# Splitting a unit's maxima before they are transposed, and two row DMAs in place of four

## The chip, the cores and the metric

The kernel runs on one core of a Trainium2 chip. The metric is the device time of one execution in microseconds; for the kernel before it is the median of three runs, 1954.19 us (1954.18 to 1955.42). Beside it stands a profiled execution of 1953.52 us, whose trace is read below.

## The reference

Two branches are mixed by a gate that is computed for each of 2048 positions (`S`); the width `D` is 640, with 32 heads of 20.

```python
def reference(A_x, A_wqkv, A_wo, B_x, B_dft_seq_re, B_dft_seq_im, B_dft_hid_re, B_dft_hid_im, gate_w):
    def _A_ref(x, wqkv, wo):
        B, S, D = x.shape
        H = 32
        Dh = D // H
        qkv = (x @ wqkv).reshape(B, S, 3, H, Dh).transpose(2, 0, 3, 1, 4)
        q, k, v = qkv[0], qkv[1], qkv[2]
        scores = jnp.einsum("bhqd,bhkd->bhqk", q, k) * (Dh ** -0.5)
        p = _softmax(scores, axis=-1)
        o = jnp.einsum("bhqk,bhkd->bhqd", p, v)
        return o.transpose(0, 2, 1, 3).reshape(B, S, D) @ wo

    def _B_ref(x, dft_seq_re, dft_seq_im, dft_hid_re, dft_hid_im):
        a = jnp.einsum("bsd,ed->bse", x, dft_hid_re)
        b = jnp.einsum("bsd,ed->bse", x, dft_hid_im)
        return jnp.einsum("ts,bse->bte", dft_seq_re, a) - jnp.einsum("ts,bse->bte", dft_seq_im, b)

    x = A_x
    g = _sigmoid((x * gate_w).sum(-1, keepdims=True))
    a = _A_ref(x, A_wqkv, A_wo)
    b = _B_ref(x, B_dft_seq_re, B_dft_seq_im, B_dft_hid_re, B_dft_hid_im)
    return g * a + (1 - g) * b
```

The inputs `A_wqkv` and `A_wo` are scaled by 64, so the scores are large and the softmax needs the maximum of each row.

## The kernel before

All large products but the attention's probabilities times the values run on TensorE in the type fp32r. To keep precision, an operand is split into two fp32r parts: `split(dst1, dst2, src, e1, e2)` (L98 to 103) copies `src`, rounded, into `dst1` (L100 on ACT, L102 elsewhere) and the rest, `src - dst1`, into `dst2` (L103).

**Units.** The attention is cut into 32 units (`NU`): a pair of heads and one half of the queries (1024). A unit has 32 steps. The keys of a pair of heads lie in `kst`, the queries in `qst`, two buffers each, with head 0 from partition 0 on and head 1 from partition 64 on. A head has 60 partitions (`KROWS`): three times 20, for the products of the two parts. Behind them come two more partitions: in `qst` they hold the negated maximum of each query in two parts, and in `kst` they hold ones. So a matmul over 62 partitions gives score minus maximum, which ACT turns into the exponential.

**The two kinds of score matmul.** An `m` (`s_mm`, L159) computes 128 queries by 512 keys over 60 partitions, only for the maximum: DVE reduces the tile to one column of `mx` (L161). An `e` (L685) computes the transposed scores, 128 keys by 512 queries over 62 partitions, and ACT takes the exponential (L687). The `m` run 41 steps (`LEAD`) ahead of the `e`. All of them, and the transpose below, take the five PSUM banks of `bank()` in turn.

**The order.** After the projections, the work is issued in cycles of four steps by the string `ORDER`, `"emFemFFFFemFeFFmeFFemFFFmmFFmeeB"`: eight `e`, eight `m`, fifteen places `F` and one burst `B`. In an `F` some pieces of other work are issued (`fill`): first the hidden transform (`hid_tile`, matmuls at L301), later the transform over the sequence (`dft_step`, matmuls at L523); `goals` says up to which piece. One `dft_step` is three pieces, and eight of them (24 pieces) use one loaded tile of the transform's matrix (`raw`, L413, from `in_cdft`); every 16th also loads earlier outputs (`yt`, L511). A burst calls `max_nm` for a unit whose maxima are complete, then `run_extras` (reading a finished output tile from `yp`, on ACT at L309 or L542, then on DVE at L310 or L543; loads of `araw`, L428; preparations on POOL), then sixteen matmuls of probabilities with values (`av`, L448), then `max_chain` for that unit.

**Steps and queues.** `begin(i)` opens step i of the `e`: it runs what `at_step` put there, and some stores. `now[0]` is the step of the latest `begin`; it is 4c + 4 in the burst of cycle c. The DMAs of `sp.dma_start` go to SP's queue in the order of the program. SP works through it as fast as the waits of each DMA allow; each DMA also waits for an earlier one to land, whose semaphore it reuses (here the one eight before). `unit_end` stores a unit's results: sums to `l_scr` (L462), back as `lc` (L465), their reciprocals (L468) to `r_scr` (L471), broadcast back as `rb` (L475), a product on POOL (L478) and the store to `o_scr` (L486). That store lies on step 25 of the next unit.

**A unit's maxima before the change.** `max_nm` (L173) reduces `mx`, 128 x 64, to `nm`, 128 x 16: for each of 128 query rows, 2 heads by 8 query tiles, negated (L175). `max_chain` (L190) transposes `nm` on TensorE into a PSUM bank, 16 x 128 (L193), and splits it there on DVE into `m1` and `m2` (L102, L103). Two steps later `rows()` writes for each head one row of 1024 from `m1` (L201) and one from `m2` (L202) into the two partitions of `qst`: four DMAs of 4 KB. For the first unit, whose maxima are computed during the projections, `rows()` follows at once.

Of the kernel before, what the change touches and what calls it, by code (L numbers as in the profile page):

```python
# [10 lines left out]
F32 = mybir.dt.float32  # L11
R = mybir.dt.float32r
AF = mybir.ActivationFunctionType
ALU = mybir.AluOpType
AX = mybir.AxisListType
# [3 lines left out]
P = 128  # L19
# [39 lines left out]
def f32(ap):  # L59
    return ap.bitcast(F32)  # L60
# [3 lines left out]
def mix_kernel(ctx: ExitStack, tc: tile.TileContext, xa, wqk, wb, cdft, wo, out):  # L64
    nc = tc.nc
    pe, act, dve, pool, sp = nc.tensor, nc.scalar, nc.vector, nc.gpsimd, nc.sync
    ctx.enter_context(tc.manual_schedule())

    def pools(**kw):
        return ctx.enter_context(tc.tile_pool(**kw))  # L70

    const = pools(name="const", bufs=1)
    small = pools(name="small", bufs=1)
# [14 lines left out]
    ident = const.tile([P, P], F32, name="ident")  # L88
# [9 lines left out]
    def split(dst1, dst2, src, e1, e2):  # L98
        if e1 is act:
            act.activation(dst1, src, AF.Copy)  # L100
        else:
            e1.tensor_copy(dst1, src)  # L102
        e2.tensor_tensor(dst2, src, f32(dst1), op=ALU.subtract)  # L103
# [8 lines left out]
    def bank():  # L112
        return ps_w.tile([P, 512], F32, name=f"ps{next(turn) % 5}")
# [24 lines left out]
    def q_unit(n):  # L138
        u = n % 2 * (S // 2)
        return qst[n // 2 % 2][:, u : u + S // 2]  # L140

    mx, nms, ends = {}, {}, []
    now, later = [-1], {}

    def at_step(i, fn):
        later.setdefault(i, []).append(fn)
# [16 lines left out]
    def s_end(i):  # L163
        n, s = divmod(i, 32)
        if n < NU and s == 31:
            if now[0] < 0:
                max_nm(n)
            else:
                ends.append(n)
        if s == 1 and 0 < n <= NU and now[0] < 0:  # L170
            max_chain(n - 1)

    def max_nm(n):  # L173
        nms[n] = small.tile([P, 16], F32, name="nm", bufs=2)
        dve.tensor_reduce(nms[n], mx.pop(n).rearrange("p h q c -> p (h q) c"), axis=AX.X, op=ALU.max, negate=True)  # L175

    def s_step(i):
        for fn in [s_mm(i, h) for h in range(2)]:
# [10 lines left out]

    def max_chain(n):  # L190
        q = q_unit(n)
        pt = bank()[:16, :P]
        pe.transpose(pt, nms.pop(n), ident)  # L193
        m1 = small.tile([16, P], R, name="m1", bufs=2)
        m2 = small.tile([16, P], R, name="m2", bufs=2)
        split(m1, m2, pt, dve, dve)

        def rows():
            for h in range(2):
                b = 64 * h + KROWS  # L200
                sp.dma_start(f32(q[b : b + 1, :]), f32(m1[8 * h : 8 * h + 8, :]))  # L201
                sp.dma_start(f32(q[b + 1 : b + 2, :]), f32(m2[8 * h : 8 * h + 8, :]))  # L202

        if now[0] < 0:
            rows()
        else:
            at_step(now[0] + 2, rows)


    pa = pools(name="att", bufs=1)  # L210
# [163 lines left out]
    for n, c in enumerate(order):  # L374
        for t in range(4):
            m = 4 * n + t
# [314 lines left out]
    def burst(c):  # L691
        for n in ends:
            max_nm(n)
        run_extras(max(done - HIDS, 0) // 3, 2)
        for kt in (2 * c, 2 * c + 1):
            av_step(now[0], kt // NS, kt % NS)
        while ends:
            max_chain(ends.pop(0))
        if c == HID - 1:
            start_dft()  # L700
# [91 lines left out]
```

## Time and profile before

| | |
|---|---|
| median of 3 runs | 1954.19 us |
| the profiled execution | 1953.52 us |
| its span, first to last instruction | 1951.7 us |
| mean granted TensorE clock | 0.997 |
| PE busy | 1918.5 us (98%) |
| DVE busy | 1454.1 us (75%) |
| ACT busy | 1211.8 us (62%) |
| POOL busy | 1045.8 us (54%) |

PE is TensorE's matmuls, PEld its weight loads, DVE VectorE, ACT ScalarE, POOL GpSimd, SP the engine whose queue issues most DMAs. A row of a timeline has the start and the duration in us, the engine, the line, the operation, what it writes and reads, the shapes, how many instructions were merged, and in brackets the idle time before it and what ended it. A row of the waits has who waited for whom, the total in us, how often, and the longest. A row of the stretches has the stretch, its length, each engine's busy time with its number of instructions (PE, PEld, DVE, ACT, POOL, or only the first of them where one line was asked for), the granted clock, the share of the DMA engines that was busy, and GB/s. A row of the groups has busy time and the mean duration in ns behind the bar, then the idle time. Ends of matmuls are modelled.

### The profile page before, as it was taken

To read this page: it belongs to the slowest core of one execution; us is meant where nothing else is said; L and a number is where in the kernel's file an instruction comes from. 1 tells how busy PE (TensorE), PEld (TensorE's weight loads), DVE (VectorE), ACT (ScalarE), POOL (GpSimd) and SP (SyncE) were. 2 spreads that over 40 slices of the span, in tenths; PEclk is the share of its full clock that TensorE was granted. 3 is DMA by queue.
4 is the path that set the end of the run, shared out by engine and by line. 5 is a ranking of instruction groups with operands and counts; after the bars stand their busy time and mean duration, and the time that the engine had idled before them with its cause. 6 is when DMAs were issued, how large, how long until landed. Compare 5 with 4: busy or idle time off the path is not lost. (4 is left out here: it accounts for less than half of the span.)

```text
span 1951.7 us, 43695 instructions
## 1 busy us (share of the span) xinstructions
PE 1918.5 (98%) x17080; PEld 1375.4 (70%) x17080; DVE 1454.1 (75%) x2419; ACT 1211.8 (62%) x2337; POOL 1045.8 (54%) x975
## 2 busy tenths in 40 slices
PE   8999999999999999999999999999999999999999
PEld 7987767777775667666666666666666666666679
DVE  4144568889887888888888878888888887888323
ACT  4221147777776676666776766676766776776741
POOL 1210001111005989457469968995786789787512
PEclk9999999999999999999999999999999999999999
DMA  7763321212114584435356746664554565454355
GB/s 224 173 172 127 130 100 46 78 61 74 47 58 141 170 228 152 122 116 149 97 173 199 196 154 189 212 177 123 149 171 125 183 169 181 154 149 147 98 165 179
DMA packets 196414, 281.02 MB, mean 144 GB/s; under 512 B 73272, under 2 KB 137816, under 8 KB 194288
## 3 DMA queue, kind: packets, MB, share of 16 engines
q1 hardware_dynamic: 158992, 246.20, 40.8%
q0 software_dynamic: 37216, 32.03, 6.7%
q8 instruction: 134, 2.20, 0.5%
q14 instruction: 72, 0.59, 0.1%
HBM read 213.81 MB, written 63.70 MB: 142 GB/s over the span
## 5 line engine op out<-in xcount | busy, mean ns | idle before, releaser
L161 DVE TENSOR_REDUCE mx<-ps 128x1 f32<-128x512 f32 x2048 | 1287.4, 683 | 197.4 <-PE ps L159 178.8
L687 ACT ACTIVATE p<-ps 128x512 f32<-128x512 f32 x2048 | 1080.9, 598 | 443.4 <-PE ps L159 241.2
L159 PE MATMUL ps<-kst,qst 60*128 60x512 f32 x2048 | 776.1, 427 | 8.0 <-DVE mx L161 3.2
L685 PE MATMUL ps<-qst,kst 62*128 62x512 f32 x2048 | 700.7, 422 | 5.8 <-DMA qst<-m 4.2
L523 PE MATMUL yp<-a,part 64*128 64x320 f32 x5376 | 687.6, 309 | 0.1
L523 PEld LDWEIGHTS yp<-a,part 64*128 64x128 f32 x5376 | 593.7, 186 | 15.3 <-DVE m L543 0.3
L448 PE MATMUL av<-p,v 128*21 128x512 f32 x4096 | 494.4, 599 | 0.1
L685 PEld LDWEIGHTS ps<-qst,kst 62*128 62x128 f32 x2048 | 335.5, 185 | 215.2 <-DVE mx L161 181.9
L159 PEld LDWEIGHTS ps<-kst,qst 60*128 60x128 f32 x2048 | 364.5, 185 | 38.2 <-DVE mx L161 11.8
L103 POOL TENSOR_TENSOR part<-raw,part 128x1024 fp32r<-128x1024 f32 x112 | 267.2, 2386 | 9.0
L448 PEld LDWEIGHTS av<-p,v 128*21 128x21 f32 x4096 | 98.3, 100 | 226.8 <-issue 223.1
L301 PE MATMUL yp<-wb,xs 64*128 64x320 f32 x1920 | 237.4, 309 | 3.7 <-ACT raw L309 3.5
L301 PEld LDWEIGHTS yp<-wb,xs 64*128 64x128 f32 x1920 | 206.8, 187 | 8.9 <-ACT raw L309 4.1
L419 POOL TENSOR_TENSOR raw<-raw,raw 128x1024 f32<-128x1024 f32 x78 | 187.4, 2402 | 17.3 <-DMA raw<-in_cdft 11.8
L102 POOL CAST part<-raw 128x1024 fp32r<-128x1024 f32 x112 | 116.4, 1039 | 116.8 <-PE yp L523 87.4
L102 POOL CAST wb<-raw 128x966 fp32r<-128x966 f32 (+1 forms) x4 | 3.4, 856 | 215.8 <-PE ps L159 215.8
L554 POOL TENSOR_TENSOR yt<-yt,m 128x320 f32<-128x320 f32 x64 | 55.5, 878 | 111.3 <-DVE m L543 104.2
L478 POOL TENSOR_TENSOR o<-o,rb 128x512 f32<-128x512 f32 x32 | 41.4, 1294 | 134.5 <-DMA rb<-r_scr 73.7
L103 POOL TENSOR_TENSOR a<-araw,a 128x320 fp32r<-128x320 f32 x112 | 97.8, 873 | 9.0
L103 DVE TENSOR_TENSOR p<-ps,p 128x512 fp32r<-128x512 f32 x40 | 27.5, 691 | 94.1 <-ACT p L100 91.4
L106 PE MATMUL ps<-xs,part 128*128 128x512 f32 x200 | 80.2, 401 | 7.8 <-ACT xs L100 6.1
L100 ACT ACTIVATE p<-ps 128x512 fp32r<-128x512 f32 x40 | 23.7, 597 | 101.4 <-PE ps L108 101.4
(67 smaller groups left out, 1331.8 us busy)
## 6 DMA issues: line engine op xcount, KB each, us to landing
raw<-in_cdft SPq DMA_DIRECT2D x192, 512.0 KB
araw<-a_scr SPq DMA_DIRECT2D x192, 160.0 KB
qk_scr<-p SPq DMA_DIRECT2D x40, 512.0 KB
kst<-qk_scr POOLq DMA_DIRECT2D x32, 320.0 KB, 12.3
qst<-qk_scr POOLq DMA_DIRECT2D x64, 160.0 KB, 8.2
a_scr<-raw SPq DMA_DIRECT2D x64, 160.0 KB
yt<-y_scr SPq DMA_DIRECT2D x64, 160.0 KB
y_scr<-yt SPq DMA_DIRECT2D x64, 160.0 KB
```

Source lines behind the costliest of these rows:

```text
L102: e1.tensor_copy(dst1, src)
L103: e2.tensor_tensor(dst2, src, f32(dst1), op=ALU.subtract)
L106: pe.matmul(ps, st1, mv1, start=first, stop=False)
L159: pe.matmul(ps, q[b : b + KROWS, qt * P : (qt + 1) * P], k[b : b + KROWS, kc * 512 : (kc + 1) * 512], start=True, stop=True)
L161: return lambda: dve.tensor_reduce(mx[n][:, h, qt, kc : kc + 1], ps, axis=AX.X, op=ALU.max)
L301: pe.matmul(yp[h][:, :HE], xs[r, xz, d, cs], w[r, wz, d, :HE], start=d == 0 and z == 0, stop=d == ND - 1 and z == 2)
L419: pool.tensor_tensor(raws[0], raws[0], raws[1], op=ALU.add if PRODUCTS[n][0][1][0] > 0 else ALU.subtract)
L448: pe.matmul(av[32 * j : 32 * j + DH + 1, :], v[:, kt, h * (DH + 1) : (h + 1) * (DH + 1)], pp[qc][:, h, :], start=kt == 0, stop=kt == NS - 1)
L523: pe.matmul(yp[h][:, :HE], c[r, cz, cs], a[r, az], start=s == 0 and z == 0, stop=s == NS - 1 and z == 2)
L554: pool.tensor_tensor(y, y, m, op=ALU.add if sg == signs[tt, hf] else ALU.subtract)
L685: pe.matmul(pt, k[b : b + KROWS + 2, kt * P : (kt + 1) * P], q[b : b + KROWS + 2, qc * 512 : (qc + 1) * 512], start=True, stop=True)
L687: act.activation(pts[n, kt, qc][:, h], pt, AF.Exp, scale=float(DH) ** -0.5)
```

## The change

`max_nm` no longer stops at `nm`. It splits it at once on DVE into two parts in a new tile `nms`, laid out per head as first part then second part, 32 columns in all. `max_chain` transposes the 32 columns together into a bank, 32 x 128, and copies the result to SBUF with one DVE instruction, into a tile `m` with one buffer. There the rows of a head, 8 of the first part and 8 of the second, lie next to each other, so one DMA of 8 KB fills both partitions of `qst` for that head. `rows()` is called three steps later in place of two.

```diff
     def max_nm(n):
-        nms[n] = small.tile([P, 16], F32, name="nm", bufs=2)
-        dve.tensor_reduce(nms[n], mx.pop(n).rearrange("p h q c -> p (h q) c"), axis=AX.X, op=ALU.max, negate=True)
+        nm = small.tile([P, 2, 8], F32, name="nm", bufs=2)
+        dve.tensor_reduce(nm, mx.pop(n), axis=AX.X, op=ALU.max, negate=True)
+        nms[n] = small.tile([P, 2, 2, 8], R, name="nms", bufs=2)
+        split(nms[n][:, :, 0], nms[n][:, :, 1], nm, dve, dve)
...
     def max_chain(n):
         q = q_unit(n)
-        pt = bank()[:16, :P]
-        pe.transpose(pt, nms.pop(n), ident)
-        m1 = small.tile([16, P], R, name="m1", bufs=2)
-        m2 = small.tile([16, P], R, name="m2", bufs=2)
-        split(m1, m2, pt, dve, dve)
+        pt = bank()[:32, :P]
+        pe.transpose(pt, f32(nms.pop(n)).rearrange("p h z q -> p (h z q)"), ident)
+        m = small.tile([32, P], F32, name="m")
+        dve.tensor_copy(m, pt)
 
         def rows():
             for h in range(2):
                 b = 64 * h + KROWS
-                sp.dma_start(f32(q[b : b + 1, :]), f32(m1[8 * h : 8 * h + 8, :]))
-                sp.dma_start(f32(q[b + 1 : b + 2, :]), f32(m2[8 * h : 8 * h + 8, :]))
+                sp.dma_start(f32(q[b : b + 2, :]), m[16 * h : 16 * h + 16, :])
 
         if now[0] < 0:
             rows()
         else:
-            at_step(now[0] + 2, rows)
+            at_step(now[0] + 3, rows)
```

## Prediction

> **What bounds the kernel now.** I read the page first, then who waited for whom on PE, then the time of single cycles, and then the timelines around the maxima and around the rows that go into `qst`.
>
> ```profile
> span 1951.7 us, 43695 instructions
> ...
> PE 1918.5 (98%) x17080; PEld 1375.4 (70%) x17080; DVE 1454.1 (75%) x2419; ACT 1211.8 (62%) x2337; POOL 1045.8 (54%) x975
> ```
> ```profile
> PE ps L106 <- ACT xs L100: 6.1, 1, 6.1
> PE ps L685 <- DMA qst<-m: 4.2, 2, 3.3
> ```
>
> PE is busy for 98% of the span, so time is gained only by taking work off PE or by ending one of its few waits. The second view lists them; two of the score matmuls (L685) waited, 4.2 us together, for the very DMAs that this change touches.
>
> Next, what a unit's maxima cost. The first pair of rows is a cycle with the transpose and the next cycle without one; the second pair is the same stretches for the filling matmuls alone.
>
> ```profile
> 1222.80:1229.11 6.31, 6.31 (x60) 4.19 (x60) 5.55 (x12) 4.20 (x8) 6.03 (x9) 1.00 0.47 130
> 1229.11:1235.17 6.06, 6.06 (x57) 4.09 (x56) 4.96 (x9) 4.18 (x8) 5.87 (x4) 1.00 0.65 217
> ```
> ```profile
> 1222.80:1229.11 6.31, 3.31 (x24) 2.72 (x24) 1.00 0.47 130
> 1229.11:1235.17 6.06, 3.27 (x24) 2.77 (x24) 1.00 0.65 217
> ```
>
> Both hold 24 fills, and PE is busy throughout both (its first number equals the length), so the 0.25 us between them is nearly all PE time. Where it goes:
>
> ```profile
> 1222.80 1.92 PE L448 MATMUL av<-p,v 128*21 128x512 f32 x16
> 1224.64 0.28 PE L193 MATMUL ps<-ident,nm 128*16 128x128 f32 x1
> 1224.85 0.49 PE L685 MATMUL ps<-qst,kst 62*128 62x512 f32 x1
> ```
> ```profile
> 1224.02 0.21 DVE L175 TENSOR_REDUCE nm<-mx 128x16 f32<-128x64 f32 x1
> 1224.95 0.28 DVE L102 CAST m<-ps 16x128 fp32r<-16x128 f32 x1 [0.72 <-PE ps L193]
> 1225.27 0.28 DVE L103 TENSOR_TENSOR m<-ps,m 16x128 fp32r<-16x128 f32 x1
> 1225.48 0.67 DVE L161 TENSOR_REDUCE mx<-ps 128x1 f32<-128x512 f32 x1
> ```
>
> The transpose starts at 1224.64 and the next matmul at 1224.85, so its place on PE is 0.21 us, of the 0.25. The two DVE instructions behind it, which the change cuts to one, are covered: PE goes on with the scores and fills while DVE does them. So shortening them gains nothing. A wait is marked before the transpose's weight load, but it is not the reduction's:
>
> ```profile
> 1224.64 0.09 PEld L193 LDWEIGHTS ps<-ident,nm 128*16 128x16 f32 x1 [0.85 <-DVE nm L175]
> ```
> ```profile
> 1026.96 0.18 PEld L685 LDWEIGHTS ps<-qst,kst 62*128 62x128 f32 x1 [0.85 <-DVE mx L161]
> ```
>
> The same 0.85 us stands after the sixteen `av` matmuls in a cycle without a transpose. It is the end of those matmuls; `nm` was finished at 1224.02 + 0.21 = 1224.23, 0.41 us before the load. That 0.41 us is the cover which the change will use.
>
> **The change part by part.**
>
> *The split ahead of the transpose.* Behind the reduction on DVE come a copy and a subtraction of 128x16, each depending on the one before. The trace has neither. The nearest row in shape is the first below; the far bound is the 0.28 us of the same two operations on 16x128 from PSUM, above.
>
> ```profile
> L390 DVE TENSOR_SCALAR gate<-gate 128x16 f32<-128x16 f32 x1 | 0.2, 165 | 0.0
> ```
> ```profile
> 1883.98 1.97 DVE part L103
> 1885.99 0.41 PE ps L108
> ```
>
> Between dependent DVE instructions lie 0.04 us (1224.95 + 0.28 = 1225.23 to 1225.27), and from DVE's end to a PE that waits also 0.04 (1883.98 + 1.97 = 1885.95 to 1885.99, on the chain that ended last). How many units this concerns stands in the waits of the weight loads:
>
> ```profile
> PEld ps L193 <- DVE nm L175: 24.6, 29, 0.8
> ```
>
> At 165 ns each the parts reach PE 0.04 + 0.165 + 0.04 + 0.165 + 0.04 = 0.45 us after the reduction: 0.04 over the cover. At 0.28 it is 0.68, or 0.27 over. Below nothing it cannot be, since the transpose already starts as soon as the `av` matmuls let it. I take 165 ns, which has the shape, and charge the 29 units of that row: 29 x 0.04 = +1.2 us; the far end is 29 x 0.27 = +7.8 us.
>
> Two things are queued behind the new pair. On PE, all of the following scores and fills wait with the transpose; that is what is charged. On DVE, in about a third of the units, it is the reading of a finished output tile:
>
> ```profile
> 1727.23 0.49 DVE L543 TENSOR_TENSOR m<-yp,m 128x320 f32<-128x320 f32 x1
> ```
> ```profile
> 1728.15 0.31 PE L523 MATMUL yp<-a,part 64*128 64x320 f32 x2
> ```
>
> It would start 0.41 later (0.45 less the last handover) and end at 1728.13, and with 0.04 to PE just meet the first fill into that tile at 1728.15. No charge, but the cover is gone too.
>
> *One transpose of 32 columns in place of 16.* The moving side stays 128 wide, so its time stays. The weight load is 0.09 us for 16 columns and 0.18 for 128; 16 more are at most 0.02 us, 32 x 0.02 = 0.6 us if it shows. I take +0.2.
>
> *One copy of 32x128.* DVE loses one instruction of 0.28 us behind the transpose and gains two of 0.165 ahead; the next maximum (L161, 1225.48) may start some 0.3 us earlier. PE waits for neither here, so 0. The bank is released earlier too; nothing waited for it.
>
> *One step later.* `rows()` moves from step now + 2 to now + 3. The burst is at step 32n - 8, so the rows move from 32n - 6 to 32n - 5. Between these two `begin` calls the order string has three F places, which run two or three fill pieces; a fill issues loads only in every 24th piece, and working out `goals` for the 31 later units gives none there. The stores `y_scr` lie on steps divisible by 4, `a_scr` on 32n - 7, and `store_o` on 32n - 7, all on the same side as before. So on SP's queue the rows pass nothing, and on POOL's they never were. SP is not paced by steps; it stops only at what a DMA needs:
>
> ```profile
> SPq L201 <- DVE m L103: 121.6, 25, 10.8
> ...
> SPq L202 <- DMA o_scr<-o: 1.4, 1, 1.4
> ```
>
> In 25 of 32 units SP stands at the rows before the split is done. There the move changes nothing.
>
> *Two DMAs for four.* This counts where SP comes late, and above all in one place:
>
> ```profile
> 1124.67 1.42 SPq L486 DMA_DIRECT2D o_scr<-o  x4
> ...
> 1127.83 0.68 SPq L201 DMA_DIRECT2D qst<-m  x1
> 1130.02 0.63 SPq L202 DMA_DIRECT2D qst<-m  x1
> 1130.70 0.64 SPq L201 DMA_DIRECT2D qst<-m  x1
> 1131.39 0.63 SPq L202 DMA_DIRECT2D qst<-m  x1
> ```
> ```profile
> 1130.35 0.31 PE L523 MATMUL yp<-a,part 64*128 64x320 f32 x1
> 1133.93 0.89 PE L685 MATMUL ps<-qst,kst 62*128 62x512 f32 x2 [3.28 <-DMA qst<-m]
> ```
>
> SP was held by a late `o_scr` store, the four row DMAs ended at 1132.02, and PE stood still for 3.28 us until 1133.93, which is 1.91 after the last issue. The second row DMA had waited 1.4 us for the landing of the first `o_scr`, eight DMAs back; with two DMAs that wait falls on the second one still. It would go out at 1130.02, end at 1130.65 and land at 1132.56: -1.37 us. If the wait fell away too, it would be about -2.8. If a two-row DMA took twice as long to issue (1.27), the gain would be nothing. I take 0.63 each, as the row has it: such a transfer is small. At the other place PE waited 0.95 us:
>
> ```profile
> 1637.89 0.77 PE L685 MATMUL ps<-qst,kst 62*128 62x512 f32 x2 [0.95 <-DMA qst<-m]
> ```
>
> Two issues of 0.63 us fewer bring the last row there at least 1.3 us forward, which takes this wait away: -0.95.
>
> The long wait has a second price, the clock (in these rows the number after the five engines; PE's busy time is the first after the length):
>
> ```profile
> 607.94:611.35 3.41, 1.83 (x18) 0.37 (x10) 0.81 (x2) 0.63 (x2) 1.78 (x1) 1.00 0.23 86
> 611.35:614.77 3.42, 2.23 (x21) 2.01 (x23) 2.09 (x4) 1.92 (x4) 3.27 (x3) 1.00 0.14 48
> ```
> ```profile
> 1130.18:1133.59 3.41, 0.47 (x6) 0.21 (x2) 2.12 (x4) 0.25 (x1) 3.27 (x3) 1.00 0.53 202
> 1133.59:1137.00 3.41, 3.07 (x14) 0.93 (x18) 0.00 (x0) 1.09 (x2) 3.35 (x3) 0.50 0.13 46
> ...
> 1618.28:1621.70 3.42, 1.37 (x14) 1.11 (x12) 1.63 (x3) 2.26 (x5) 3.28 (x5) 1.00 1.01 306
> 1621.70:1625.11 3.41, 3.07 (x18) 2.32 (x22) 2.27 (x4) 0.35 (x1) 3.27 (x3) 0.50 0.92 265
> ```
>
> After a stretch with 0.47 or 1.37 us of PE work the next one ran at half clock; after one with 1.83 it did not. Half clock over 3.07 us of work costs at most 1.5. A wait shorter by 1.37 leaves 1.9 us idle, that is 1.5 us of work if all of it falls into one stretch, between the two cases, and more if it straddles two. I count the dip as gone, narrowly: -1.5; kept, it is 0.
>
> The Trainium skill (TensorE: Matmul & The Clock Gate, Part 1) says that the gate looks at free-running windows of 3413 ns and goes to half rate after an idle one. The rows agree on the length, but a window with 1.37 us of work was enough here. By the page the dip would surely go, with the same sum as mine; by the rows it is open.
>
> The sum: +1.2 + 0.2 - 1.37 - 0.95 - 1.5 = -2.4 us. The profiled execution took 1953.52 us (its span 1951.7 and 1.8 around it), so 1951.1; the median of the three runs is 0.67 above that execution, which gives 1951.8.
>
> **The rivals.** I count as no change what lies within 0.2%, 3.9 us (1950.3 to 1958.1), about what a measurement of this kernel can tell.
>
> *Slower: the transpose starts late.* The parts of the maxima become what PE waits for in each unit. For it: the cover is 0.41 us and three handovers alone are 0.12. Against it: the row with the same shape. At 0.28 us each the sum is +7.8 + 0.2 - 3.8 = +4.2, so 1958.4. It decides against the change from a delay of 0.26 us a unit on (29 x 0.26 = 7.5, less 3.6).
>
> *No gain from the DMAs.* The two-row DMA lands as late as the four did: longer to issue, or fewer engines carrying it. Then the waits and the dip stay, and +1.4 is left: 1955.6. For it: no DMA in the trace has this form. Against it: 8 KB either way, and 0.63 us for each issue of 4 KB in all rows above.
>
> The Trainium skill (DMA: Bandwidth & Descriptors, "Why a DMA increments its semaphore by 16 and not by 1") has a rule that points there: a DMA uses the largest number of engines, at most 16, that divides the slowest dimension of both sides. Sixteen partitions against two rows would get 2 engines, where eight partitions could get 8. No row here shows the engines of one DMA.
>
> *A larger gain.* The long wait shrinks by 2.8 since the wait for `o_scr` falls away as well, the dip goes, and the parts stay inside the cover: -2.8 - 1.5 - 0.95 + 0.2 = -5.1, so 1949.1. For it: two DMAs fewer in each unit stand in the queue of eight.
>
> **How the numbers follow.** The forecast (1951.8) gets 0.5; its own range, with the dip kept or gone and the delay from 0 to 0.08 us, is 1950.5 to 1954. The larger gain gets 0.2, no gain 0.15, slower 0.15. The range must leave out no more than 0.2, half of the slower case and part of the larger gain: 1949.0 to 1957.5. Faster by over 0.2% is the larger gain, 0.20; slower is the late transpose, 0.15; the rest, 0.65, is within 0.2%.
>
> **What would show it.** Right: copy and subtraction on 128x16 near 165 ns; the transposes' start at most 0.1 us later after the burst than 1224.64 - 1222.80 = 1.84; 64 row DMAs near 0.63 us; the wait of L685 for `qst` under 2 us in all, and one stretch less at half clock. Wrong: the transpose 2.1 us or more after the burst's start; row DMAs of over 1 us; new waits of POOL or PE for loads that this working left in place.

## The result and the profile after

The changed kernel takes 1987.7 us (median of 5 runs, 1979.35 to 1991.91); the kernel before took 1955.42 us beside it. The ratio is 1.0159, with an interval from 1.0131 to 1.0188: 1.6% slower, outside the predicted range. The profiled execution took 1979.35 us. Its page has these first lines:

```profile
span 1977.6 us, 43619 instructions
...
PE 1921.5 (97%) x17080; PEld 1379.5 (70%) x17080; DVE 1482.4 (75%) x2451; ACT 1212.3 (61%) x2337; POOL 1046.1 (53%) x975
```

PE has nearly the same work (3 us more), but the span is 25.9 us longer. DVE has 32 instructions more and is busy for 28.3 us longer, almost 0.9 us for each one added. What PE waited for (who waited for whom: us in total, times, longest) begins with a line that before did not have:

```profile
PE ps L195 <- DVE nms L103: 22.7, 17, 3.3
...
PE ps L685 <- DMA qst<-m: 2.6, 1, 2.6
```

The transpose waits for the second part of the maxima, 22.7 us in 17 of the 32 units. The wait for the row DMAs fell from 4.2 to 2.6 us; the prediction had named under 2 as its sign. It is the smaller matter. The pair over all 32 units, and the reduction ahead of it (duration in ns, least, median, greatest; then when, and the shape):

```profile
L102 DVE CAST nms<-nm x32: 174/176/2189, 223.0 to 1849.9; 128x16 fp32r<-128x16 f32 x32
L103 DVE TENSOR_TENSOR nms<-nm,nms x32: 174/175/2264, 223.2 to 1850.1; 128x16 fp32r<-128x16 f32 x32
```
```profile
L175 DVE TENSOR_REDUCE nm<-mx x32: 208/210/221, 222.8 to 1849.6; 128x16 f32<-128x64 f32 x32
```

42 of the 64 instructions of the pair take 174 to 176 ns, near the 165 that the forecast assumed. The other 22 take up to 2.3 us for 16 elements per partition. The reduction is never long, though 17 of the 32 lie wholly within an instruction of POOL. The worst unit shows what goes with the long ones. First DVE, then POOL, then PE, in the same stretch:

```profile
1185.54 0.21 DVE L175 TENSOR_REDUCE nm<-mx 128x16 f32<-128x64 f32 x1
1185.78 1.37 DVE L102 CAST nms<-nm 128x16 fp32r<-128x16 f32 x1
1187.18 2.26 DVE L103 TENSOR_TENSOR nms<-nm,nms 128x16 fp32r<-128x16 f32 x1
```
```profile
1184.77 2.35 POOL L103 TENSOR_TENSOR part<-raw,part 128x1024 fp32r<-128x1024 f32 x1
1187.08 2.34 POOL L419 TENSOR_TENSOR raw<-raw,raw 128x1024 f32<-128x1024 f32 x1
```
```profile
1184.31 1.92 PE L448 MATMUL av<-p,v 128*21 128x512 f32 x16
1189.50 0.28 PE L195 MATMUL ps<-ident,nms 128*32 128x128 f32 x1 [3.28 <-DVE nms L103]
```

The copy starts at 1185.78, while an instruction of POOL is under way, and ends at 1187.15; that instruction ended at 1187.12. POOL's next one begins at 1187.08, before the subtraction at 1187.18; the subtraction ends at 1189.44, POOL's at 1189.42. So each of the two DVE instructions ended some 0.03 us after the POOL instruction that had started ahead of it, and the transpose came 5.19 us after the start of the `av` burst, against 1.84 before. Over the whole trace, 20 of the 22 long instructions ended 0.03 to 0.04 us after a POOL computation; the other two are taken up at the end of this document. In the eight units whose maxima fell before 630 us no POOL computation ran beside the pair, and all sixteen instructions took 174 to 176 ns.

The stretch from one `av` burst to the next, with the transpose in it, shows the loss by stage (mean us, worked out from the starts of the bursts on PE's timeline; the columns are the cycles with 24, 30 and 32 fills, of which there are 13, 6 and 10; two more with a transpose, the one at 617 us without fills and the last, are left out and differ by less than 0.1 us from before to after; those with 30 fills lie in the hidden transform, where POOL is idle beside them):

| kernel | 24 | 30 | 32 |
|---|---|---|---|
| before | 6.338 | 6.478 | 6.517 |
| after | 7.553 | 6.552 | 7.610 |
| copy_sbuf | 7.060 | 6.503 | 7.016 |
| copy_psum | 6.403 | 6.492 | 6.515 |
| after_psum_b | 6.504 | 6.556 | 6.562 |
| dma_two_b | 6.465 | 6.479 | 6.516 |
| before_late | 6.587 | 6.609 | 6.679 |
| after_late | 6.820 | 6.841 | 8.269 |

From before to after: 13 x 1.215 + 6 x 0.074 + 10 x 1.093 = 27.2 us, slightly more than the 25.9 by which the span grew. The cycles without a transpose have the same medians in both kernels. So the loss is in these 29 cycles, and nearly all of it where POOL works. (The means for 24 fills of copy_psum, after_psum_b and dma_two_b hold the cycle near 1624 us, which ran in part at half clock in these executions and took 7.33, 8.01 and 8.05 us, against 6.49 in before.)

The cycles lost more than the 22.7 us of waiting. In part this is the clock: behind the two longest holds, at 670 and 1185 us, PE ran on at half clock for one stretch each. In these rows the granted clock is the third number from the end:

```profile
674.60:678.00 3.40, 3.40 (x23) 3.37 (x22) 2.22 (x5) 2.76 (x5) 3.33 (x3) 0.50 0.50 145
1190.00:1193.40 3.40, 3.40 (x23) 3.13 (x23) 2.22 (x5) 2.16 (x4) 0.00 (x0) 0.50 0.29 99
```

The theory (*port*): DVE and POOL share a way to SBUF which one of them holds for a whole instruction; a DVE copy from SBUF to SBUF, and a DVE operation with two inputs in SBUF, must wait for it; the reduction does not. The rows above show who ended when; a rule of the Trainium skill says the same (SBUF — State Buffer, "🔬 SBUF: two separate sides"): "The shared pair is an **exclusive lock**, not a bandwidth split". The trace agrees, with 2264 ns against 174. The rivals: two more dependent steps are too long for the cover, whatever POOL does; the place of the transpose or of the rows in the order; the new form of DMA.

### The profile page after: what moved, and what is told of

Its sections match the earlier page's. It is cut to its first block, busy times and chain, and to the rows that moved or that the text cites. A ratio compares the mean times of both kernels' runs of the same rounds, so it can differ in the third digit from the quotient of the medians.

```text
span 1977.6 us, 43619 instructions
## 1 busy us (share of the span) xinstructions
PE 1921.5 (97%) x17080; PEld 1379.5 (70%) x17080; DVE 1482.4 (75%) x2451; ACT 1212.3 (61%) x2337; POOL 1046.1 (53%) x975
## 4 chain that ended last, share of the span: by engine, by line
PE 82%; DVE 7%; DMA 6%; issue 2%; POOL 2%; ACT 1%; SPq 0%; POOLq 0%; DVEq 0%; ACTq 0%
PE av L448 20%; PE yp L523 17%; PE ps L685 15%; PE ps L159 11%; PE yp L301 6%; DVE mx L161 5%; PE ps L106 4%; PE ps L108 4%; PE ps L107 4%; DMA raw<-in_cdft 2%; DVE nms L102 1%; DMA v<-v_scr 1%; DMA kst<-qk_scr 1%; DMA lc<-l_scr 1%; POOL raw L419 1%
## 5 line engine op out<-in xcount | busy, mean ns | idle before, releaser
L103 POOL TENSOR_TENSOR part<-raw,part 128x1024 fp32r<-128x1024 f32 x112 | 267.3, 2386 | 9.0
L419 POOL TENSOR_TENSOR raw<-raw,raw 128x1024 f32<-128x1024 f32 x78 | 186.9, 2396 | 17.3 <-DMA raw<-in_cdft 10.7
L103 POOL TENSOR_TENSOR a<-araw,a 128x320 fp32r<-128x320 f32 x112 | 97.8, 873 | 9.0
L103 DVE TENSOR_TENSOR p<-ps,p 128x512 fp32r<-128x512 f32 x40 | 27.5, 691 | 93.9 <-ACT p L100 91.2
```

Of the source, the lines that this page charges most:

```text
L419: pool.tensor_tensor(raws[0], raws[0], raws[1], op=ALU.add if PRODUCTS[n][0][1][0] > 0 else ALU.subtract)
```

## The experiments

Each ratio is against the kernel before, run beside it on the same chip: 1958.52 us for the first four, 1955.4 for the next three, 1960.06 for the last three.

**One copy more.** Before, with a copy of the maxima ahead of the transpose, SBUF to SBUF:

```diff
+        nm = small.tile([P, 16], F32, name="nm", bufs=2)
...
+        nms[n] = small.tile([P, 16], F32, name="nmc", bufs=2)
+        dve.tensor_copy(nms[n], nm)
```

> The kernel before, with one DVE copy of nm, 128x16, from SBUF to SBUF ahead of the transpose, which takes the copy; the split behind the transpose and the four row DMAs stay. Port theory (a DVE copy within SBUF cannot run while a POOL instruction works on SBUF): the copy takes 0.175 us while POOL is idle and up to 2.2 us else, the transpose waits in about half of the units of the later part, 10 to 18 us slower than before. Length theory (more dependent steps overrun the cover of 0.41 us, POOL has no part): one step of 0.175 and 0.04 fits the cover, no change. DMA theory (the row DMAs or their step cost the time): no change.

Measured: 1971.32 us, ratio 1.0061 (1.0042 to 1.0080). The copy, and PE's wait for it:

```profile
L177 DVE COPY nmc<-nm x32: 174/274/2316, 221.6 to 1842.7; 128x16 f32<-128x16 f32 x32
```
```profile
PE ps L195 <- DVE nmc L177: 11.6, 13, 1.9
```

**The same copy, read from PSUM.** The reduction writes `nm` into free columns of the transpose's bank, and the copy takes it from there (all units but the first):

```diff
+            banks[n] = bank()
+            nm = banks[n][:, 256:272]
...
+        nms[n] = small.tile([P, 16], F32, name="nmc", bufs=2)
+        dve.tensor_copy(nms[n], nm)
...
-        pt = bank()[:16, :P]
+        pt = (banks.pop(n) if n in banks else bank())[:16, :P]
```

> As copy_sbuf, but the reduction writes nm into a free part of the PSUM bank that the transpose uses (but for the first unit), so the copy reads PSUM. Port theory: the copy takes the same 0.15 to 0.2 us in every unit, whatever POOL does, and the kernel is within 2 us of before. Length theory: as copy_sbuf. A theory by which any further DVE instruction is stretched there (by DMAs landing, or by PE's load): as slow as copy_sbuf, 10 us or more.

Measured: 1961.48 us, ratio 1.0000 (0.9984 to 1.0016); the median itself is 3 us above that of before. The 31 copies:

```profile
L181 DVE COPY nmc<-ps x31: 173/174/175, 313.8 to 1832.6; 128x16 f32<-128x16 f32 x31
```

No matmul of PE waited for one of them. The same work at the same place, depending on the same reduction, costs nothing that can be measured once its input isn't in SBUF. So one more step by itself isn't what costs.

**The subtraction alone.** Before, with `nm` minus a tile of zeros, both in SBUF, ahead of the transpose:

```diff
+    zeros = const.tile([P, 16], F32, name="zeros")
+    pool.memset(zeros, 0.0)
...
+        nms[n] = small.tile([P, 16], F32, name="nmc", bufs=2)
+        dve.tensor_tensor(nms[n], nm, zeros, op=ALU.subtract)
```

> As copy_sbuf, but in place of the copy DVE subtracts a tile of zeros from nm, two inputs in SBUF. Port theory with two SBUF inputs counting as well: as copy_sbuf, 8 to 18 us slower, with single subtractions of up to 2.3 us. If only copies are concerned and the long subtractions of the changed kernel were the copy's wait: 0.175 us in every unit and no change.

Measured: 1971.8 us, ratio 1.0058 (1.0041 to 1.0074).

```profile
L179 DVE TENSOR_TENSOR nmc<-nm,zeros x32: 174/176/2334, 220.5 to 1843.4; 128x16 f32<-128x16 f32 x32
```
```profile
PE ps L197 <- DVE nmc L179: 12.2, 12, 1.9
```

Two inputs in SBUF cost as much as a copy. Either part of the pair alone costs about 0.6%; the unit at 1185 shows how both can pay in the same unit.

**The DMAs alone.** Before, with two row DMAs of 8 KB, each for one part and both heads:

```diff
-            for h in range(2):
-                b = 64 * h + KROWS
-                sp.dma_start(f32(q[b : b + 1, :]), f32(m1[8 * h : 8 * h + 8, :]))
-                sp.dma_start(f32(q[b + 1 : b + 2, :]), f32(m2[8 * h : 8 * h + 8, :]))
+            qq = q.rearrange("(h r) c -> h r c", h=2)
+            sp.dma_start(f32(qq[:, KROWS]), f32(m1))
+            sp.dma_start(f32(qq[:, KROWS + 1]), f32(m2))
```

> The kernel before with two row DMAs of 8 KB (one for each part, both heads in one) in place of four; the split stays behind the transpose. Port theory: the DMAs are no part of the loss; 1 to 4 us faster than before, with the wait of L685 for qst under 3 us. DMA theory: most of the loss is here, 15 us or more slower.

Measured: 1951.62 us, ratio 0.9964 (0.9944 to 0.9984): faster than both kernels. It was run once more, below.

**The whole change, with the maxima in PSUM.** After, but the reduction writes `nm` into the transpose's bank, so that the copy and the subtraction have at most one input in SBUF (all units but the first). The rows stay at three steps:

```diff
-        nm = small.tile([P, 2, 8], F32, name="nm", bufs=2)
+        if now[0] < 0:
+            nm = small.tile([P, 2, 8], F32, name="nm", bufs=2)
+        else:
+            banks[n] = bank()
+            nm = banks[n][:, 256:272].rearrange("p (h q) -> p h q", h=2)
...
-        pt = bank()[:32, :P]
+        pt = (banks.pop(n) if n in banks else bank())[:32, :P]
```

> The changed kernel, with the reduction writing nm into a free part of the PSUM bank that the transpose uses (but for the first unit): the copy then reads PSUM, and the subtraction has one input in PSUM and one in SBUF. Port theory: both take about 0.175 us in every unit, no transpose waits over 0.1 us, the loss is gone and the gain of the two DMAs is left: 1 to 8 us faster than the kernel before. Length theory: as slow as the changed kernel, 20 us or more over before.

Measured: 1956.32 us, ratio 1.0007 (0.9994 to 1.0020). The loss of 1.6% is gone, with the two dependent steps and the change's own two DMAs still in place; so neither of these is the loss. The expected gain over before did not show here, which led to the repeat below.

**The transpose later.** After, with `max_chain` two steps behind the burst, so that the pair has time, and the rows one step after that:

```diff
-            max_chain(ends.pop(0))
+            at_step(now[0] + 2, functools.partial(max_chain, ends.pop(0)))
...
-            at_step(now[0] + 3, rows)
+            at_step(now[0] + 1, rows)
```

> The changed kernel, with the transpose and its copy issued two steps after the burst in place of within it, and the rows one step after that, the same step as in the changed kernel. Port theory: copies and subtractions still take up to 2.3 us each, but some 2 us of scores and fills lie between them and the transpose, so PE waits for the parts in at most 3 units, and the kernel is between 8 us faster and 4 us slower than before. A theory by which PE's loss comes from DVE being held (the maxima are reduced late, banks come free late): still 10 us or more slower than before.

Measured: 1981.47 us, ratio 1.0131 (1.0110 to 1.0152). My first expectation missed: moving what waits for the pair wins little. The second, by which the loss comes from DVE being held, forecast 10 us or more, and it was 26. PE's waits:

```profile
PE yp L523 <- DVE m L543: 7.4, 4, 2.4
PE ps L195 <- DVE nms L103: 7.1, 5, 2.3
```

The transpose waits less, 7.1 in place of 22.7 us. But DVE itself is still held, and what is queued behind the pair on it comes late. The timelines of DVE, POOL and PE in the cycle at 773 us:

```profile
776.21 0.66 DVE L102 CAST nms<-nm 128x16 fp32r<-128x16 f32 x1
776.90 2.27 DVE L103 TENSOR_TENSOR nms<-nm,nms 128x16 fp32r<-128x16 f32 x1
779.09 0.48 DVE L543 TENSOR_TENSOR m<-yp,m 128x320 f32<-128x320 f32 x1
```
```profile
776.79 2.34 POOL L419 TENSOR_TENSOR raw<-raw,raw 128x1024 f32<-128x1024 f32 x1
```
```profile
779.62 0.41 PE L523 MATMUL yp<-a,part 64*128 64x320 f32 x1 [2.41 <-DVE m L543]
```

The subtraction is let go with POOL's end, then DVE reads the output tile, and PE has stood still for 2.41 us for that tile. This is the queue behind the pair which the prediction named and didn't charge.

**The rows earlier.** After, with `rows()` at step now + 2 as in before:

```diff
-            at_step(now[0] + 3, rows)
+            at_step(now[0] + 2, rows)
```

> The changed kernel with the rows two steps after the burst, as before, in place of three. Port theory, and the working by which the rows pass nothing on the queue: within 4 us of the changed kernel, some 25 to 32 us slower than before. If the later step costs something: faster than the changed kernel by 5 us or more.

Measured: 1982.11 us, ratio 1.0138 (1.0109 to 1.0167), the same as after within both intervals; the wait for `nms` was 26.0 us in 18 units. The later step costs nothing that can be measured.

**The later place without the pair.** Before, with `max_chain` two steps behind the burst: the place of after_late, with no new work on DVE.

```diff
-            max_chain(ends.pop(0))
+            at_step(now[0] + 2, functools.partial(max_chain, ends.pop(0)))
...
-            at_step(now[0] + 2, rows)
+            at_step(now[0] + 1, rows)
```

> Before, with the transpose and its split put two steps after the burst of av instead of right behind it (the row DMAs then go out one step later than in before). It carries no new work on VectorE, so it prices the place alone. If the place costs nothing and the loss of after_late is VectorE being held while GpSimd works: within 3 us of before, transposed cycles at 6.34, 6.48 and 6.52 us as in before. If the place in the middle of a cycle costs by itself: in after_late the 30-fill cycles, where GpSimd is idle, were 0.36 us longer than before's; over 29 units that is 10 us, 5 to 13 us slower than before, and the rest of after_late's loss (some 14 us) is VectorE's.

Measured: 1965.83 us, ratio 1.0040 (1.0027 to 1.0054). The place costs by itself, in all three kinds of cycle: 13 x 0.249 + 6 x 0.131 + 10 x 0.162 = 5.6 us. PE also waited longer for the rows, but so it did in copy_psum, where the rows go out as in before; the lines of before_late, then copy_psum:

```profile
PE ps L685 <- DMA qst<-m: 7.9, 3, 4.9
```
```profile
PE ps L691 <- DMA qst<-m: 7.6, 3, 4.7
```

So that wait can't be put down to the place. What is left of after_late, 1.0131 against 1.0040 or some 18 us, goes with the pair; the two waits quoted there show 14.5. Of the rest, 6 x 0.232 = 1.4 us lie in the cycles with 30 fills, where POOL is idle, and are not its hold.

**The DMAs and the PSUM form side by side.** Both once more on one chip, in more rounds.

> dma_two once more, to be read on one chip beside after_psum_b. If two DMAs for four are worth by themselves what dma_two showed: 4 to 10 us faster than before (ratio 0.995 to 0.998). If that was a lucky set of runs: within 2 us of before.

> after_psum once more beside dma_two_b: the change as it was meant, without what GpSimd does to it. By the port theory with the prediction's sum: 29 units at 0.03 to 0.08 us for the part of copy and subtraction that outlasts its cover make it 1 to 2.5 us slower than dma_two_b, so still 2 to 8 us faster than before. If the split ahead of the transposes costs more than that by itself: level with before, 5 us or more above dma_two_b.

Measured: dma_two_b 1949.58 us, ratio 0.9955 (0.9943 to 0.9967); after_psum_b 1956.04 us, ratio 0.9983 (0.9972 to 0.9994). The pair's instructions in after_psum_b:

```profile
L102 DVE CAST nms<-ps x31: 173/174/175, 313.6 to 1831.0; 128x16 fp32r<-128x16 f32 x31
L103 DVE TENSOR_TENSOR nms<-ps,nms x31: 173/174/175, 313.8 to 1831.2; 128x16 fp32r<-128x16 f32 x31
```

So the gain of two DMAs held a second time, and the version with the old split behind the transpose stays ahead. The means of the cycles give the pair 13 x 0.039 + 6 x 0.077 + 10 x 0.046 = 1.4 us against dma_two_b. The medians differ by 6.5, which is the expectation's other case, a split that costs more by itself; but the cycles with a transpose do not show such a cost. In the profiled executions 4.5 us of the 10.8 between the spans lie in one cycle at 608 us, where PE waits for ACT, ACT for POOL and POOL for a load of `in_cdft`. That cycle took 6.85 and 7.21 us in dma_two and dma_two_b, 8.51 and 11.69 in after_psum and after_psum_b, and 9.64 in before. So dma_two has something there that the change has not; whether it is the form of the DMAs (one two-row DMA for each head, against one for each part) stays open, since no run parted the form from the pair.

## Why the prediction was wrong, by its steps

**What bounds, and the cover.** Right: PE bounds; the cover is 0.41 us, and at 174 ns each the pair overruns it by 0.06. In after_psum_b, where nothing holds the pair, its cycles are 0.04 to 0.08 us longer than dma_two_b's, 1.4 us in all. As far as the cycles show it, that is the +1.2 +0.2 of the sum.

**The split ahead of the transpose.** This is the step that failed. It took 165 ns from row L390, and 0.28 us as the far end. L390 had the right shape and the wrong circumstances, since it ran at 271 us with POOL idle; the 0.28 us were of instructions on 16x128 that read PSUM. Neither has a DVE instruction between two tiles in SBUF beside a running POOL, which is what the change adds 64 times. The working asked how long each step takes, and not what DVE would have to wait for. In their place stood 695 ns for the copy and 380 for the subtraction, as means over 32 units:

```profile
L102 DVE CAST nms<-nm 128x16 fp32r<-128x16 f32 x32 | 22.2, 695 | 1.1
```
```profile
L103 DVE TENSOR_TENSOR nms<-nm,nms 128x16 fp32r<-128x16 f32 x32 | 12.2, 380 | 1.1
```

Less 174 each that is 23.3 us of standing still, near PE's new wait of 22.7. A better far end would have been a whole POOL instruction for each, 2.4 us, as L419 and L103 take. The trace of before had the hint, in the very instruction whose end was quoted for the 0.04 us of a handover. In its timelines of DVE and POOL:

```profile
1883.90 2.04 DVE L103 TENSOR_TENSOR part<-raw,part 128x640 fp32r<-128x640 f32 x1
...
1886.78 0.81 DVE L103 TENSOR_TENSOR part<-raw,part 128x640 fp32r<-128x640 f32 x1
```
```profile
1882.12 3.14 POOL L727 TENSOR_SCALAR p<-p,ngate 128x640 f32<-128x640 f32 x4
```

The same operation on the same shape took 2.04 and then 0.81 us. The first began while POOL was in the third of its four instructions; the last of them ended at 1885.26, and 0.68 us later the subtraction was done. A duration two and a half times another of the same form should have been asked for its cause. The Trainium skill (SBUF — State Buffer, "Who interferes with whom") names both forms, copies and casts in the two-port mode and operations with two inputs in SBUF; the prediction weighed rules on the clock and on DMAs, and not this one.

**The rival "the transpose starts late".** It had the right mechanism for PE, and its point of decision held: 0.26 us a unit was passed, with 22.7 / 29 = 0.78. But its price went by the same far end, so that 1958.4 was the most it could give; the kernel came out 29 us above that. Its chance of 0.15 was weighed by row shapes alone.

**The transpose of 32 columns, the one copy, the later step.** Right: the weight load takes 93 to 97 ns against 86 to 88 for 16 columns, and the step costs nothing that can be measured (after_step2). That the rows pass no DMA was not quite so: in the units at 316, 416 and 622 us two load DMAs (`in_wb` or `araw`) stood ahead of them which stand behind them in after_step2.

**Two DMAs for four.** Right in sign. With four row DMAs PE waited for them 4.2 us in before and 2.1, 3.3 and 7.6 in copy_sbuf, sub_sbuf and copy_psum; with two it was 2.6 in after, 2.9 and 1.7 in dma_two and dma_two_b, and 1.6 to 1.9 in after_psum, after_psum_b and after_step2. The forecast left 1.9. The issues in after:

```profile
L202 SPq DMA_DIRECT2D qst<-m x64: 616/634/804, 235.4 to 1853.5; - x64
```

0.63 us, as taken. The dip of the clock, which the forecast called narrow, went both ways. In after it stayed, behind a stretch with 0.79 us of PE work:

```profile
1142.20:1145.60 3.40, 0.79 (x8) 0.45 (x10) 1.77 (x3) 0.16 (x1) 3.26 (x3) 1.00 0.81 309
1145.60:1149.00 3.40, 3.40 (x18) 0.48 (x10) 0.00 (x0) 0.92 (x2) 3.40 (x2) 0.50 0.02 6
```

So the -1.5 was not won there. dma_two kept this dip as well, dma_two_b did not, and the two cycles from 1125 us on took 16.9 and 14.0 us in these two executions of one kernel, against 17.1 in before: 0.2 and 3.1 us won of the 2.9 forecast for that place. At 1616 to 1638 us dma_two won 1.6, dma_two_b lost 0.7.

The medians gained more than the forecast's -1.37 - 0.95 - 1.5 = -3.8 us: -6.9 and -10.5 (-3 to -11, and -6.5 to -11 by the intervals). Two things stand behind the difference. The traced execution of before took 1953.52 us, less than its medians beside dma_two and dma_two_b, 1958.52 and 1960.06. And both executions of dma_two won 2.4 to 2.8 us in the cycle at 608 us, which no term of the forecast has. SP issued the two loads of `in_cdft` there without the hold that they had in before (first before, then dma_two); the next issue was held in their place.

```profile
599.61 1.50 SPq L413 DMA_DIRECT2D raw<-in_cdft  x2
```
```profile
599.91 0.81 SPq L412 DMA_DIRECT2D raw<-in_cdft  x2
```

In the nine other traces this cycle took 8.2 to 12.8 us, so it is hardly chance; no row DMA stands near, and how two DMAs bring it about is open.

## What to carry to other kernels

The price of a small instruction is that of its neighbours: before adding a VectorE copy between two SBUF tiles, or an operation with two inputs in SBUF, look at what GpSimd runs at that moment, and take a whole GpSimd instruction as the far end. Where it matters, let the operation read PSUM, which cost 173 to 176 ns here in all 31 units. And when one instruction in a trace takes twice what its twin takes, ask why before using it as a row.

## What the runs showed of the hardware that was not expected

Two dependent DVE instructions don't pass as one: POOL's next instruction, which began at 1187.08 us, before the copy's end, held the subtraction too, and the pair paid twice (1.37 + 2.26 us). Both were long in four of the 32 units.

A DMA that POOL issues can hold DVE as well. Timelines of POOL and DVE in after:

```profile
1239.14 1.30 POOL L478 TENSOR_TENSOR o<-o,rb 128x512 f32<-128x512 f32 x1
1240.38 0.57 POOL L635 DMA_DIRECT2D qst<-qk_scr  x1
```
```profile
1240.17 0.75 DVE L102 CAST nms<-nm 128x16 fp32r<-128x16 f32 x1
```

The copy ended at 1240.92, not behind the product (1240.44) but with the end of the issue (1240.95). The copy at 723.83 us did the same: it waited out a product and then an issue, 1.75 us in all, so one DVE instruction can pay for two of POOL's. But the subtraction at 1650.53 us took its 174 ns in the middle of an issue (1650.41 to 1651.04). No run tested the issue alone, and when it holds is open.
